# Fewer weight chunks in flight, a later scan of the second batch's v, and a new order of the first transfers

## The chip, the cores and the metric

The kernel runs on one core of one Trainium2 chip. The metric is the device time of one execution in microseconds (us); the number quoted is the median of several executions.

## What is computed

An attention layer whose scores get a learned relative-position bias, followed by a gated feed-forward block. Cut to what matters:

```python
scores = scale * np.matmul(q, k.transpose(0, 1, 3, 2))        # 4 batches, 8 heads, 576 x 576, head_dim 64
psi_rel = np.log1p(np.abs(rel)); psi_i = np.log1p(np.maximum(pos[:, None], 1.0))
h = np.maximum((psi_rel / psi_i)[..., None] @ w1 + b1, 0.0)   # hidden 32
attn = softmax(scores + (h @ w2).transpose(2, 0, 1))          # one bias per head, the same for all batches
x = (attn @ v)                                                # as 2304 tokens x 512
out = ((x @ w_a) * (x @ w_b)) @ w_out                         # d_ff 1536; the weights are float64
```

## The kernel before

All of it is one program on one core. The position bias is made first, in units of 16 query rows, and stored to a buffer in HBM (`bias_d`), from which each attention tile later loads its 128 rows. The first 16 units are made in the opening stage (lines 825 to 831): the log table `u` is scaled by `w1` (line 129), four rectified copies of it are made on VectorE and ScalarE (lines 143 and 147), TensorE contracts them (line 153, tile `psta`), ScalarE evicts (lines 169 and 172) and GpSimd issues the store to `bias_d` (line 174). Ten matmuls on a constant tile (`keep`, line 820, tile `pr`) stand ahead of the first unit on TensorE; the constant is written by one GpSimd memset (line 815).

Attention goes over 160 tiles of up to 128 query rows, n = 0, 1, 2, ... in `attn_steps` (line 615). Tile n's soft-max is issued in step n; the loads for a head pair ("unit" in `attn_steps`) are asked for some tiles ahead of its first tile: q and k six tiles, v four, the preparation of q and k three, and that of v one. The first 12 units (`NF`) use v as it is loaded (`whole`, tile `rvw`); the later ones split it.

For each batch, `v_scale` (line 209) scans the four v tiles of that batch for their largest size: it loads them once more (tile `rv`, two buffers), takes absolute sums on ScalarE (line 220), reduces them on VectorE (line 228), has TensorE turn the result (line 77, tile `vm` to `pr`), and spreads a power-of-two scale two steps later (line 90). `VS` says at which tile each batch's scan begins; for batch 1 it is tile 12, one call a tile, so that its turn on TensorE stands in step 17.

The 24 chunks of `w_a` and `w_b`, 512 KB of float64 each, are loaded and turned into two half-precision parts by `wab_steps` (line 318), interleaved with the attention steps: in its step s, chunk s is converted (line 264 on ScalarE, lines 266, 267 and 270 on VectorE), its size is taken one step later (line 287), and its parts are made seven steps later (lines 304 to 308, GpSimd and ScalarE). The raw chunks have six buffers. `fetch_to` asks for chunks ahead: at step s for all up to number `s + min(6, 3 + s // 2)`, where number s has just been converted.

TensorE's order is written out by hand through `merge`; the other engines' instructions, SyncE's transfers among them, are put in order by a scheduler that simulates the program. `paced` keeps a load behind the bias rows that were asked for last, and `late` keeps work on VectorE, ScalarE and GpSimd behind the newest soft-max instructions. From about 95 us on, the feed-forward matmuls (line 690, tile `ab`; line 739, tile `o`) fill TensorE between the attention tiles.

Of the kernel before, what the change touches and what calls it, by code (L numbers as in the profile page):

```python
# [43 lines left out]
N0 = 4 * NP  # L44
# [1 line left out]
NU0 = TOK // 16  # L46
W0 = 4
NF = 3 * NP
VS = N0 - 4, 2 * N0 - 4, 3 * N0 - 10


@with_exitstack
def attention_moe(ctx, tc, q0d, q1d, kd, vd, idn, wp, wa, wb, wo, lsw, lg, rl, out):
    nc = tc.nc
# [4 lines left out]
    att = ctx.enter_context(tc.tile_pool(name="att", bufs=1))  # L59
# [43 lines left out]
    tab = {}  # L103

    def bias_tables():
        wps = cst.tile([128, 10], F32, name="wps")
        nc.sync.dma_start(out=wps, in_=wp)
        lgs = cst.tile([128, S // 4], F32, name="lgs")
        nc.scalar.dma_start(out=lgs, in_=lg)
        rls = cst.tile([128, NU], F32, name="rls")  # L110
        nc.scalar.dma_start(out=rls, in_=rl)
        w2s = cst.tile([128, 32], F32, name="w2s")
        nc.vector.memset(w2s, 0.0)
        for r in range(4):
            sl = slice(32 * r, 32 * r + 32)
            nc.vector.tensor_scalar(
                out=w2s[sl, 8 * r:8 * r + 8], in0=wps[sl, 2:10], scalar1=-1.0, scalar2=None, op0=ALU.mult
            )
        nc.vector.tensor_scalar(out=lgs, in0=lgs, scalar1=wps[:, 1:2], scalar2=None, op0=ALU.mult)
        tab["w1"], tab["w2"], tab["b1l"], tab["rl"] = wps[:, 0:1], w2s, lgs, rls  # L120

    def bias_windows(pool, tag):
        u = pool.tile([128, S], F32, tag=tag, name="u", bufs=1)
        nc.sync.dma_start(out=u, in_=lsw)
        return u
# [192 lines left out]
    def wab_steps(wt):  # L318
        np_ = FC // 2
        raws, wfs, ms, dgs, rms = {}, {}, {}, {}, {}  # L320

        def fetch(i):
            pool = wtp[0] if i % 2 else wt
            raws[i] = pool, w_load(pool, (wa, wb)[i % 2], i // 2)

        ahead = [0]

        def fetch_to(n):
            for i in range(ahead[0], min(n, 4 * np_)):
                fetch(i)  # L330
                ahead[0] = i + 1

        fetch_to(3)
        yield
        for s in range(4 * np_ + 7):
            p, c = divmod(s - 7, 4)
            if 0 <= p < np_:
                if c == 0:
                    rms[p] = wab_scale(p, pow2_up(dgs.pop(p), 4, "w"))
                with late():  # L340
                    wab_parts(p, c, wfs.pop(s - 7), rms[p])
            p, c = divmod(s - 5, 4)
            if 0 <= p < np_ and c == 0:
                dgs[p] = pow2_down(ms.pop(p), 4, "w")
            if 1 <= s <= 4 * np_:
                p, c = divmod(s - 1, 4)
                if c == 0:
                    ms[p] = wtp[1].tile([128, 4], F32, tag="wm", name="wm", bufs=2)
                wab_size(2 * p + c // 2, c % 2, wfs[s - 1], ms[p])
            if s < 4 * np_:  # L350
                wfs[s] = wab_conv(s, *raws.pop(s))
                fetch_to(s + 1 + min(6, 3 + s // 2))
            yield

    def wo_steps(wt):
# [259 lines left out]
    def attn_steps():  # L615
        vgen = [None]
        for n in range(NT + 3):
            u = TILES[n][0] if n < NT else None
            if n == 0:
                qk_pair(0)  # L620
            if n + 4 < N0:
                load_bias(n + 4)
            elif N0 <= n + 2 < NT:
                load_bias(n + 2)
            if n < NT:
                soft1(n)
            for _ in range(stream[1].count(2 * n)):
                next(stream[0], None)
            for ahead, un in ((a, TILES[n + a][0]) for a in (6, 4, 3, 1) if n + a < NT and FIRST[TILES[n + a][0]] == n + a):
                if un < NP:  # L630
                    continue
                if ahead == 6:
                    load_unit(un)
                elif ahead == 4:
                    b, hp, c = UNITS[un]
                    st["raw", un] = *st["raw", un][:2], load_v(b, hp, whole=un < NF)
                elif ahead == 3:
                    with late():
                        prep_k(un)
                        prep_q(un)  # L640
                else:
                    if un == B * NP:
                        v_tail()
                    with late():
                        prep_v(un)
            if n in VS:
                vgen[0] = v_scale(VS.index(n) + 1)
            if vgen[0]:
                next(vgen[0], None)
            yield  # L650
            for _ in range(stream[1].count(2 * n + 1)):
                next(stream[0], None)
            if n + 1 < N0 + 2:
                if n % 2:
                    qk_pair(n + 1)
            elif n + 1 < NT:
                qk(n + 1, qkp)
            if n == B * N0 + 1:
                chunk_pool(1)
            if n >= 2 and n - 2 < NT:  # L660
                turn(n - 2, tpp)
            if n == N0 + 1:
                pv_first(n - 2, pvp)
            elif n >= 3 and n - 3 < N0:
                if TILES[n - 3][1][0] == "B" and n != N0 + 2:
                    pv_first(n - 3, pvp)
            elif n >= 3 and (n - 2 >= NT or TILES[n - 3][0] != TILES[n - 2][0]):
                pv(TILES[n - 3][0], pvp)
            if 1 <= n <= NT:
                soft2(n - 1)  # L670
            yield
# [131 lines left out]
    with tc.tile_pool(name="bg", bufs=1, side="right") as bg, tc.tile_pool(name="eq", bufs=1, space=PSUM) as eq, \  # L803
            tc.tile_pool(name="prp", bufs=1, space=PSUM) as prp[0]:
        epool[:] = bg, eq
        bias_tables()
        tab["idn"] = cst.tile([128, 128], F32, name="idn")
        nc.scalar.dma_start(out=tab["idn"], in_=idn)
        tab["one"] = wtmp.tile([4, 128], F32, name="one")
        nc.vector.memset(tab["one"], 1.0)  # L810
        uls = bias_windows(att, "rk")
        bias_scale(uls)

        busy = w16t[:, FC - 1, 0, 0].rearrange("p k n -> p (k n)")
        nc.gpsimd.memset(busy, 1.0)

        def keep(n):
            ps = pr_tile()
            for _ in range(n):
                nc.tensor.matmul(ps, busy[:, 0:128], busy, start=True, stop=True)  # L820

        spare = w16t[:, 2:].rearrange("p f j x k n -> p (f j x k n)").bitcast(F32)
        hrows = spare[:, :16 * S].rearrange("p (b g n) -> p b g n", b=4, g=4)

        def first_units(banks):
            for un in range(NU0):
                h4 = hrows[:, un % 4]
                hs = bias_relu(lambda g: h4[:, g], uls, un, int(un % 2 == 0 or un >= 8))
                keep((10, 2, 2, 2, 1, 1, 1)[un] if un < 7 else 0)
                bias_unit(bh, lambda: banks(un), un, hs, 6, nc.gpsimd)  # L830
                yield

        def first_loads():
            for un in range(NP):
                load_unit(un)
                prep_k(un)
                prep_q(un)
                yield
            for un in range(NP):
                b, hp, c = UNITS[un]  # L840
                st["raw", un] = None, None, load_v(b, hp, True)
                prep_v(un)
                yield

        def two(un):
            return (qkp, eq)[un % 2].tile([128, 2, 512], F32, tag="qk", name="psta", bufs=1)

        fl = first_loads()
        ws = ctx.enter_context(ExitStack())
        wtp[0] = ws.enter_context(tc.tile_pool(name="wty", bufs=1, reuse_waits="tile"))  # L850
        with tc.tile_pool(name="bh", bufs=1, side="right") as bh:
            units = first_units(two)
            merge((units, NU0 // 2), (fl, 2 * NP))
            next(wts)
            for m in range(4):
                load_bias(m)
            merge((units, NU0 // 2), (v_scale(0), 7), (wts, 2))
        keep(8)
        merge((asteps, 4), (wts, 1), ((keep(2) for _ in range(4)), 4))
        merge((asteps, 2 * N0 - 10), (wts, 7))  # L860
        n0 = 2 * ends[0] - 2 * N0 + 6
        merge((asteps, n0), (wts, 3), ((keep(2) for _ in range(n0)), n0))
# [32 lines left out]
    with tc.tile_pool(name="bg2", bufs=1, reuse_waits="tile") as bg:  # L895
        uls = bias_windows(bg, "u")
# [70 lines left out]
```

## Time and profile before

| what | value |
|---|---|
| median of 3 runs | 793.14 us (791.31 to 797.51) |
| profiled execution, its own time | 791.7 us |
| its span, from the first to the last instruction | 789.9 us |
| granted TensorE clock, mean | 0.998 |
| TensorE busy | 756.0 us, 96% of the span |
| VectorE, ScalarE, GpSimd busy | 65%, 63%, 41% |
| transfers | 114.15 MB, mean 145 GB/s |

A busy share is a mean over the whole span; a wait in one stage is read from that stage. PE is TensorE's matmuls, PEld its weight loads, DVE VectorE, ACT ScalarE, POOL GpSimd, SP SyncE, which issues most transfers. "Idle before" in a row is the time for which the engine stood still ahead of that instruction, and behind the arrow is what ended it.

### The profile page before, as it was taken

How to read it: one execution, taken by the hardware profiler on the slowest of the kernel's cores; microseconds unless marked ns; L12 is line 12 of the kernel's file. 1: busy time of each engine (PE TensorE's matmuls, PEld its weight loads, DVE VectorE, ACT ScalarE, POOL GpSimd, SP SyncE). 2: the span in 40 equal slices, each digit the busy share in tenths (PEclk: the TensorE clock that was granted, in tenths of full speed). 3: DMA queues.
4: the chain of work that ended last, by engine and by line, in shares of the span. 5: the costliest groups of instructions: out<-in, count | busy, mean ns of one | idle time of the engine just before them, and what ended most of it. 6: DMA issues, size and time to landing. Idle time of an engine off the chain costs nothing.

```text
span 789.9 us, 16363 instructions
## 1 busy us (share of the span) xinstructions
PE 756.0 (96%) x5939; PEld 601.1 (76%) x5939; DVE 509.6 (65%) x1203; ACT 500.1 (63%) x1086; POOL 321.9 (41%) x493
## 2 busy tenths in 40 slices
PE   7778899998999999999999999999999999999998
PEld 1245566677876676888888889888988888888886
DVE  7688688589975787658777877777776662110100
ACT  6879787878866787657775776567666663421310
POOL 3448667946742233224443344234433443320200
PEclk9999999999999999999999999999999999999999
DMA  8999575678645545444444443444344211100001
GB/s 258 319 363 320 181 229 177 200 238 266 200 123 171 159 138 154 122 151 124 125 142 144 145 125 109 129 145 125 109 134 141 77 54 54 48 1 27 2 14 40
DMA packets 52979, 114.15 MB, mean 145 GB/s; under 512 B 6564, under 2 KB 10916, under 8 KB 52900
## 3 DMA queue, kind: packets, MB, share of 16 engines
q1 hardware_dynamic: 45744, 97.35, 39.0%
q10 hardware_dynamic: 5876, 10.93, 4.7%
q0 software_dynamic: 1280, 4.84, 1.8%
q8 instruction: 47, 0.77, 0.4%
q14 instruction: 32, 0.26, 0.1%
HBM read 95.91 MB, written 17.18 MB: 143 GB/s over the span
## 4 chain that ended last, share of the span: by engine, by line
PE 72%; DVE 8%; ACT 6%; issue 4%; DMA 4%; POOL 3%; SPq 1%; ACTq 0%; DVEq 0%; POOLq 0%
PE ab L690 27%; PE o L739 19%; PE qk L468 8%; PE tp L545 8%; PE pv L594 6%; PE psta L153 3%; DVE p L496 2%; DMA bias<-bias_d 2%; ACT p L501 1%; DVE wt L270 1%; DMA rv<-vd 1%; DVE w16t L267 1%; POOL wos L312 1%; DMA rvf<-vd 1%; DVE w16t L266 1%
## 5 line engine op out<-in xcount | busy, mean ns | idle before, releaser
L690 PEld LDWEIGHTS <-w16t 128*128 128x128 f16 x2592 | 250.6, 98 | 41.7 <-issue 13.3
L690 PE MATMUL ab<-x,w16t 128*128 128x256 f16 x2304 | 270.1, 273 | 0.4 <-DVE g L700 0.3
L532 POOL TENSOR_SCALAR p<-p,sm 128x576 f32<-128x576 f32 x144 | 125.9, 874 | 65.3 <-DVE sm L530 57.7
L496 DVE CUSTOM_DVE_ANT_0 p<-qk,bias 128x576 f32<-128x576 f32 x144 | 108.3, 754 | 60.9 <-PE tp L545 55.0
L501 ACT ACTIVATE p<-p,mn 128x576 f32<-128x576 f32 x144 | 111.7, 776 | 40.8 <-DVE mn L496 39.8
L739 PE MATMUL o<-wos,gh 128*128 128x512 f32 x384 | 123.2, 402 | 0.0
L715 POOL TENSOR_TENSOR gl<-g,gh 128x256 fp32r<-128x256 f32 x96 | 71.8, 748 | 121.5 <-ACT gh L714 120.1
L529 POOL TENSOR_SCALAR sm<-sm 128x1 f32<-128x1 f32 x144 | 32.1, 223 | 198.4 <-ACT p L501 194.6
L568 ACT CAST pt<-tp 128x640 f16<-128x640 f32 x96 | 66.3, 691 | 70.8 <-PE tp L545 70.2
L545 PE MATMUL tp<-idn,p 128*128 128x128 f32 x720 | 104.5, 276 | 6.8 <-ACT ptf L550 4.2
L545 PEld LDWEIGHTS tp<-idn,p 128*128 128x128 f32 x720 | 83.4, 141 | 20.6 <-issue 8.4
L700 DVE SCALAR_TENSOR_TENSOR g<-ab,wv,asb 128x256 f32<-128x256 f32 x84 | 40.4, 481 | 79.1 <-ACT asb L698 78.3
L739 PEld LDWEIGHTS o<-wos,gh 128*128 128x128 f32 x384 | 68.9, 188 | 16.2 <-issue 3.3
L468 PE MATMUL qk<-ks,qs 128*128 128x288 f32 x384 | 73.0, 312 | 5.2 <-DVE mn L496 5.1
L739 PE MATMUL o<-wos,gl 128*128 128x512 f32 x192 | 75.4, 393 | 0.0
L468 PEld LDWEIGHTS qk<-ks,qs 128*128 128x128 f32 x384 | 56.6, 190 | 14.3 <-DVE mn L496 7.1
L698 ACT ACTIVATE asb<-ab,wv 128x256 f32<-128x256 f32 x84 | 39.3, 468 | 38.3 <-PE ab L690 38.1
L572 DVE TENSOR_TENSOR pt<-tp,pt 128x512 f16<-128x512 f32 x80 | 55.1, 689 | 8.0 <-ACT pt L568 7.9
L714 ACT CAST gh<-g 128x256 fp32r<-128x256 f32 x96 | 38.8, 404 | 33.9 <-DVE g L700 33.7
L530 DVE RECIPROCAL sm<-sm 128x1 f32<-128x1 f32 x144 | 23.3, 162 | 44.1 <-POOL sm L529 43.1
L400 DVE TENSOR_TENSOR ks<-rk,ks 64x576 fp32r<-64x576 f32 x48 | 44.7, 932 | 4.5 <-ACT ks L399 1.7
L739 PEld LDWEIGHTS o<-wos,gl 128*128 128x128 f32 x192 | 36.0, 188 | 8.2
(107 smaller groups left out, 1033.3 us busy)
## 6 DMA issues: line engine op xcount, KB each, us to landing
bias<-bias_d SPq DMA_DIRECT2D x128, 288.0 KB, 2.9
rv<-vd SPq DMA_DIRECT2D x32, 320.0 KB, 3.3
rk<-kd SPq DMA_DIRECT2D x24, 288.0 KB, 3.4
wraw<-wa SPq DMA_DIRECT2D x12, 512.0 KB, 6.9
wraw<-wb SPq DMA_DIRECT2D x12, 512.0 KB, 5.1
wraw<-wo SPq DMA_DIRECT2D x12, 512.0 KB, 4.3
bias_d<-bo ACTq DMA_DIRECT2D x20, 295.5 KB, 3.0
rq<-q1d SPq DMA_DIRECT2D x16, 320.0 KB, 3.8
```

The lines of the kernel that those rows point to most:

```text
L400: nc.vector.tensor_tensor(out=ks[ol, j], in0=rk[sl], in1=ks[sl, j].bitcast(F32), op=ALU.subtract)
L468: nc.tensor.matmul(ps[:, hf, :HB], a, b[:, hf * HB:hf * HB + HB], start=(x == 0), stop=(x == len(prods) - 1))
L496: ttr = nc.vector.tensor_tensor_reduce(out=p.rearrange("p (a n) -> p a n", a=2), in0=ps[:, :, :HB], in1=bt.rearrange("p (a n) -> p a n", a=2),
L501: exps.append(nc.scalar.activation(p, p, AF.Exp, bias=mn, scale=-1.0, accum_out=sm))
L532: nc.gpsimd.tensor_scalar(out=p, in0=p, scalar1=rc, scalar2=1.0, op0=ALU.mult, op1=ALU.mult)
L545: nc.tensor.transpose(tp[:, x, :], p[:, c0:c0 + 128], tab["idn"])
L568: nc.scalar.copy(dst[:, 0:5], src)
L572: nc.vector.tensor_tensor(out=dst[:, 5:9], in0=src[:, 0:4], in1=dst[:, 0:4], op=ALU.subtract)
L594: nc.tensor.matmul(ps[64 * j:64 * j + 64, :N], v[:, j, :], p[:, j * N:j * N + N], start=(x == 0), stop=(x == len(prods) - 1),)
L690: nc.tensor.matmul(ab[:, j], w16[nm, f][:, pw, kk, :], xs[px][:, kk, :], start=(x % (3 * KC) == 0), stop=(x % (3 * KC) == 3 * KC - 1),)
L715: nc.gpsimd.tensor_tensor(out=gl, in0=g, in1=gh.bitcast(F32), op=ALU.subtract)
L739: nc.tensor.matmul(o, g[:, sl], wos[f][:, p], start=(f == 0 and x == 0), stop=(f == FC - 1 and x == 2))
```

## The change

Four edits. The log table is loaded ahead of everything else on SyncE's queue; the small table `wps` moves from SyncE's to ScalarE's queue, ahead of `lg` and `rl`; and the identity matrix, which came third on ScalarE's queue, is issued by GpSimd. The scan of the second batch's v starts at tile 14 in place of tile 12. Weight chunks are asked for at most 4 steps ahead in place of 6 (the formula differs from step 4 on). The v tiles of units 4 to 11 are asked for three tiles ahead in place of four.

```diff
-VS = N0 - 4, 2 * N0 - 4, 3 * N0 - 10
+VS = N0 - 2, 2 * N0 - 4, 3 * N0 - 10
...
-        nc.sync.dma_start(out=wps, in_=wp)
+        nc.scalar.dma_start(out=wps, in_=wp)
...
-                fetch_to(s + 1 + min(6, 3 + s // 2))
+                fetch_to(s + 1 + min(4, 3 + s // 2))
...
                 if ahead == 6:
                     load_unit(un)
-                elif ahead == 4:
+                elif ahead == (4 if un >= NF else 3):
                     b, hp, c = UNITS[un]
                     st["raw", un] = *st["raw", un][:2], load_v(b, hp, whole=un < NF)
-                elif ahead == 3:
+                if ahead == 3:
                     with late():
                         prep_k(un)
                         prep_q(un)
-                else:
+                elif ahead == 1:
...
+        uls = bias_windows(att, "rk")
         bias_tables()
         tab["idn"] = cst.tile([128, 128], F32, name="idn")
-        nc.scalar.dma_start(out=tab["idn"], in_=idn)
+        nc.gpsimd.dma_start(out=tab["idn"], in_=idn)
         tab["one"] = wtmp.tile([4, 128], F32, name="one")
         nc.vector.memset(tab["one"], 1.0)
-        uls = bias_windows(att, "rk")
         bias_scale(uls)
```

## Rows read from the trace of the kernel before

**Rows 1.** Busy time of each engine over the whole span.
```profile
PE 756.0 (96%) x5939; PEld 601.1 (76%) x5939; DVE 509.6 (65%) x1203; ACT 500.1 (63%) x1086; POOL 321.9 (41%) x493
```
**Rows 2.** Busy time by stage, clock, share of the transfer engines, GB/s.
```profile
28.00:100.00 72.00, 60.18 (x463) 35.66 (x464) 51.17 (x149) 57.86 (x136) 42.96 (x63) 1.00 0.84 291
100.00:230.00 130.00, 122.13 (x949) 94.52 (x946) 107.27 (x241) 102.56 (x224) 91.30 (x109) 0.99 0.67 211
230.00:670.00 440.00, 438.51 (x3569) 367.23 (x3566) 315.90 (x727) 291.68 (x622) 156.23 (x279) 1.00 0.42 126
```
**Rows 3.** The same view in stretches of 6 us: PE, PEld, DVE, ACT, POOL.
```profile
70.00:76.00 6.00, 5.67 (x52) 3.44 (x48) 4.38 (x15) 5.59 (x16) 4.53 (x7) 1.00 0.99 330
76.00:82.00 6.00, 5.21 (x39) 2.87 (x36) 4.51 (x15) 6.00 (x16) 3.63 (x7) 1.00 0.82 285
82.00:88.00 6.00, 4.89 (x38) 2.78 (x37) 4.00 (x13) 3.87 (x10) 3.97 (x6) 1.00 0.61 201
```
**Rows 4.** Timeline of the start: us from the start, duration, instruction, idle before.
```profile
0.75 0.39 SPq L107 DMA_DIRECT2D wps<-wp  x1
1.20 0.42 SPq L124 DMA_DIRECT2D u<-lsw  x1
1.32 3.84 PE L820 MATMUL pr<-w16t 128*128 128x512 f16 x10 [1.32 <-POOL w16t L815]
...
3.37 0.30 DVE L119 TENSOR_SCALAR lgs<-lgs,wps 128x144 f32<-128x144 f32 x1
4.34 0.52 DVE L129 TENSOR_SCALAR u<-u,wps 128x576 f32<-128x576 f32 x1 [0.68 <-DMA u<-lsw]
...
5.48 1.54 PE L153 MATMUL psta<-w16t,w2s 128*32 128x288 f32 x8 [0.32 <-DVE w16t L143]
```
**Rows 5.** GpSimd's transfer issues: first one, all 16 (ns min/median/max); VectorE beside it.
```profile
L174 POOL DMA_DIRECT2D bias_d<-bo x1: 4222/4222/4222, 9.5 to 9.5; - x1
L174 POOL DMA_DIRECT2D bias_d<-bo x16: 530/575/4222, 9.5 to 35.0; - x16
4.90 8.65 DVE L143 TENSOR_SCALAR w16t<-u,lgs 128x576 f32<-128x576 f32 x21
```
**Rows 6.** Timeline around the end of batch 1's scan.
```profile
78.75 0.38 SPq L205 DMA_DIRECT2D rv<-vd  x1
...
84.22 0.74 ACT L220 ACTIVATE rv<-rv 128x640 f32<-128x640 f32 x1 [1.30 <-DMA rv<-vd]
84.86 0.19 ACT L220 ACTIVATION_READ_ACCUMULATOR rv<-rv 128x1 f32 x1
85.39 0.38 PE L77 MATMUL pr<-idn,vm 128*1 128x128 f32 x2 [0.74 <-DVE vm L228]
86.13 0.59 PE L820 MATMUL pr<-w16t 128*128 128x512 f16 x2 [0.37 <-DVE p2m L79]
```
**Rows 7.** Weight chunks: SyncE's wait (us, times, longest), VectorE's wait, landing times, conversions.
```profile
SPq L258 <- DVE w16t L267: 16.0, 12, 2.5
...
48.40 0.76 DVE L496 CUSTOM_DVE_ANT_0 p<-qk,bias 128x576 f32<-128x576 f32 x1 [1.92 <-DMA bias<-bias_d]
...
DMA to landing us min/median/max: 3.8/5.7/11.9
...
DMA to landing us min/median/max: 4.5/4.6/5.2
...
115.48 1.11 DVE L267 SCALAR_TENSOR_TENSOR w16t<-wraw,w16t 128x512 int32<-128x512 int32 x1
126.24 0.67 ACT L264 ACTIVATE wt<-wraw 128x512 f32<-128x512 f32 x1
```
**Rows 8.** The first use of a moved v tile on TensorE.
```profile
111.50 2.53 PE L594 MATMUL pv<-ptw,rvw 128*64 128x256 f32 x20
```
**Rows 9.** One stall of TensorE at 195 us, and its stretch by the stage view.
```profile
195.60 1.33 PE L468 MATMUL qk<-ks,qs 128*128 128x288 f32 x4 [2.58 <-DVE mn L496]
...
195.00:200.00 5.00, 4.40 (x24) 3.91 (x25) 3.95 (x11) 4.42 (x10) 3.82 (x5) 0.66 0.76 262
```

## Prediction

> **What bounds the kernel now.** I read the engines' totals first, then the busy time by stage, then the chain of waits and the timeline of the stages that the edits touch. TensorE is busy for 96% of the span [rows 1], and the stage view says where the rest is: from 230 to 670 us it is busy 438.51 us of 440, so nothing that is done to transfers there can be bought back; from 100 to 230 us it lacks 7.9 us, and from 28 to 100 us it lacks 11.8 us [rows 2]. The edits act between 0 and 135 us, so the most they could give is a part of those 11.8 and 7.9 us and of the opening. What is saved early passes on to the end, since later work follows in a fixed order on TensorE; what is saved inside another engine's slack is lost. The transfers are near full between 34 and 76 us (a share of 0.99 in 70 to 76) and far from full after 82 us (0.61) [rows 3]. That picture suits the change, but a full transfer queue costs only where an engine stands waiting for it. In all of 28 to 260 us only two waits of an engine over half a microsecond were ended by a transfer: VectorE once 1.92 us for bias rows [rows 7], and ScalarE once 1.30 us for a v tile [rows 6]. That small sum is why I expect little.
>
> **The opening.** The log table's issue moves from 1.20 to 0.75 us on SyncE [rows 4], 0.45 earlier. VectorE waits for that table now (0.68 us ahead of 4.34). The table `lg` goes the other way: it was first on ScalarE's queue and is second now, one issue of 0.45 later. VectorE's instruction on it at 3.37 did not wait, so `lg` had landed by then; at worst it lands at 3.82, and with that instruction's 0.30 us the table is scaled from 4.12 on. So the scaling starts 0.22 to 0.45 us earlier, and the first real matmul, at 5.48 behind VectorE, could start at 5.03 to 5.26. But the ten constant matmuls stand ahead of it on TensorE and end at 1.32 + 3.84 = 5.16 [rows 4], which leaves a gain of 0.2 to 0.3. The constant comes from GpSimd, and the identity's issue now stands ahead of that memset in the program. The trace shows no identity issue on GpSimd; the nearest rows are its 16 bias stores, which hold it for 0.53 us at least and 0.575 in the median, with one of 4.22 [rows 5]. At 0.53 to 0.75 the ten matmuls end at 5.69 to 5.91, 0.2 to 0.4 us later than the first real matmul starts today. If the scheduler puts the memset first, it is -0.3; if the issue takes 4.22 us, the ten matmuls end at 9.38, and it is 9.38 - 5.48 = +3.9. I take +0.3, by the median row, because 4.22 has a cause beside it that is missing at 0.75 us: VectorE ran without a gap from 4.90 to 13.55, and that store, begun at 9.45, ended at 13.67 [rows 5]. The moves of `wps` and `rl` cost nothing: `wps` is issued at the same 0.75 us, and `rl` is first used by the eviction behind the first `psta` matmuls.
>
> The page SBUF — State Buffer of the Trainium skill (section "SBUF: two separate sides") has a rule on this: a transfer issued by GpSimd has its descriptors written by GpSimd itself, and VectorE can lock it out of the port that it needs for that until VectorE's instruction is done. The 4.22 us store beside VectorE's run agrees with it. By that rule the identity's issue is a short one and the sum below stands at -1.7; by the reading that GpSimd's first issue is slow in itself, the sum is +1.9.
>
> **The scan of batch 1's v, two tiles later.** Today its last tile is asked for at 78.75 us and read from 84.22 on, 5.4 us later; ScalarE waits 1.30 us for it; TensorE, whose order is fixed, waits 0.74 us for the reduced result and 0.37 us for its small successor [rows 6]. Two tiles later the loads fall where the transfer share is 0.61 at most [rows 3], so I count both waits as gone: -1.1 us (bounds 0 and -1.1). What TensorE meets next is the score matmul of the following tile, whose operands have been there long. Second, ScalarE is the fullest engine between 70 and 82 us, 11.59 us of 12, and idle for 2.1 us of the 6 behind that [rows 3]. The other three of the four absolute sums lie in the full stretch, each like the fourth, 0.74 + 0.19 = 0.93 us [rows 6]. Two of them move out: 1.9 us of ScalarE's work goes to where it has room. The chain there changes between ScalarE, VectorE, GpSimd and TensorE, so I count half, -0.9 us (bounds 0 and -1.9). The scale itself is ready in step 21 in place of 19, and its first reader is the eviction behind the matmuls at 111.50 [rows 8], in the second half of step 22: covered, by less than two steps. Were that cover gone, VectorE and TensorE would wait a few tenths of a microsecond there.
>
> **Chunks at most 4 steps ahead.** It removes no transfer; from step 4 on each chunk is asked for up to two steps later. With 6 ahead and 6 buffers, SyncE stands at each request until the chunk just being converted has been read: 16.0 us in 12 waits [rows 7]. With 4 ahead that buffer has been free for two steps, so these waits go. Queued behind them are bias rows and v tiles, but their readers hardly wait, so I count 0. It could be better by the 1.92 us that VectorE waited for bias rows [rows 7]; against that, the rows which landed at 48.3 were issued at 39.2, before the first chunk that moves (asked for near 45 us). It could be worse where steps are shortest: the chunk converted at 126.24 would be asked for once the conversion at 115.48 has ended at 116.59, 9.65 us before its use. Landings take 5.2 us at most after 95 us, and 11.9 at most in the full stretch [rows 7]: cover of 4.4 us, or a loss of 2.3 at the worst. I take 0, as the late rows are the nearer ones.
>
> **v of units 4 to 11, one tile later.** Each is asked for ten tiles ahead of its first matmul (four ahead of its unit, used six into it), where that of the first stands at 111.50 [rows 8]; one tile less is covered many times over, and from unit 6 on the load waits for its buffer anyway. It is 0.
>
> **The sum.** +0.3 - 1.1 - 0.9 + 0 + 0 = -1.7 us. Against the profiled execution that is 791.7 - 1.7 = 790.0 (span 788.2). The median of the runs lies 1.4 above it, so 793.14 - 1.7 = 791.4.
>
> **The rivals.** (a) GpSimd's first issue is slow in itself: in place of +0.3 it is +3.9, the sum is +1.9, 795.0, slower than before. It decides from an issue of about 2.2 us on, where the opening eats the other two gains. For it: the only first issue in the trace took 4.22. Against it: that issue ended when VectorE's run did. (b) The scheduler's new order removes the stall at 195 us. There VectorE did weight conversions ahead of a soft-max step, TensorE stood for 2.58 us, and then ran in a stretch with a granted clock of 0.66, that is, part of it at the lower level of 1.2 GHz; its four score matmuls took 1.33 us for the usual 0.77, and with the five transposes and 36 feed-forward matmuls behind them some 1.7 us more were lost [rows 9]. Without it: -4.3, 787.1. (c) The same in the other direction: the order of conversions puts one more such stall there: 795.7. Nothing in the edits aims at 195 us, so both are chance. (d) The scan's waits only move with it to step 19, where feed-forward matmuls queue behind them: the -1.1 is not had, 792.5. Against it: the transfers are half idle there. (e) The chunk edit opens the full stretch between 34 and 76 us after all, VectorE's 1.92 us go: 789.5.
>
> **How the numbers follow.** Chances: the forecast 0.45, (a) 0.13, (b) 0.13, (c) 0.11, (d) 0.10, (e) 0.08. The forecast's own range is 788.5 to 794.0. The range for all must take in (b) with some of (e) below and (c) above, and the runs of one kernel reach from 791.31 to 797.51 by themselves: 785.5 to 797.0. A change of 1%, 7.9 us, is about what a measurement of this kernel can tell from none. Faster than that needs (b), (e) and the full 1.9 us of ScalarE together: 0.08. Slower than that needs (a), (c) and a late chunk together: 0.05. Same: 0.87.
>
> **What the profile will show.** Right: the first `psta` matmul between 5.1 and 5.9 us; GpSimd's identity issue near 0.6 us; no wait of TensorE at line 77 for `vm`, whose turn comes near 94 us; two absolute sums fewer before 82 us; SyncE's waits at line 258 for line 267 nearly gone; TensorE still at about 756 us busy. Wrong: a `psta` near 9 us, a wait for `wraw` at line 264, `vm` still waited for, or TensorE's idle time between 100 and 230 us off by several microseconds, which would be the order of VectorE and not the edits' own waits.

## The result: slower, and the profile after

The changed kernel takes 799.16 us (median of 15 runs, 794.75 to 801.37) against 793.14 us for the kernel before (15 runs, 790.94 to 797.51): a ratio of 1.0065, with a 95% interval of 1.0048 to 1.0082, that is 5.2 us more (3.8 to 6.5). Forecast were 791.4 us and a range of 785.5 to 797.0, so the sign was wrong, and the time lies above the range. The profiled execution of the changed kernel took 800.78 us, 9.1 more than the one of before; it lies near the top of its kernel's runs, so its trace shows more of the loss than the median has.

The engines' totals, and the busy time by stage with the clock in the seventh column, answer to [rows 1, 2]; the stretches of 10 us stand ahead of the three stages.

```profile
PE 763.1 (96%) x5939; PEld 604.3 (76%) x5939; DVE 508.8 (64%) x1203; ACT 500.4 (63%) x1086; POOL 324.6 (41%) x494
```

```profile
10.00:20.00 10.00, 5.22 (x40) 0.96 (x36) 5.51 (x15) 6.72 (x19) 5.29 (x3) 0.83 0.97 333
...
50.00:60.00 10.00, 7.02 (x36) 4.05 (x32) 4.48 (x15) 5.68 (x14) 1.87 (x4) 0.66 0.83 294
60.00:70.00 10.00, 9.13 (x73) 6.35 (x71) 7.72 (x21) 8.02 (x20) 5.32 (x8) 0.82 0.77 254
70.00:80.00 10.00, 7.25 (x62) 5.32 (x61) 8.09 (x22) 8.56 (x20) 8.92 (x12) 0.86 0.82 252
...
28.00:100.00 72.00, 58.94 (x415) 33.93 (x416) 46.92 (x134) 54.98 (x131) 41.93 (x58) 0.91 0.82 279
100.00:230.00 130.00, 122.96 (x937) 93.39 (x936) 106.97 (x248) 102.09 (x221) 91.13 (x109) 0.99 0.67 212
```

TensorE ran the same 5939 matmuls and was busy 7.1 us longer. The stage rows show a lower granted clock in 10 to 20 us and from 50 to 80 us, where the trace of the kernel before had 1.00 throughout; the twenty `pv` matmuls at 59.77 us took 2.60 us there in place of 1.46. In 28 to 100 us it did 415 matmuls in place of 463, while its busy time fell by only 1.2 us. From 100 to 230 us the row is nearly that of before, so most of the time went early.

The places where one instruction stands for the same work show how the lag grew. First before, then after: the last constant matmuls of the opening, the `pv` matmuls that stand at 57.99 us before, the score matmul that stands at 120.27 us before, behind the turn of `vm` in both kernels, and, of after alone, that turn.

```profile
33.62 1.90 PE L820 MATMUL pr<-w16t 128*128 128x512 f16 x8
57.99 1.46 PE L513 MATMUL pv<-ptf,rvf 128*64 128x128 f32 x20
120.27 1.24 PE L468 MATMUL qk<-rkf,rqf 64*128 64x288 f32 x4
```

```profile
35.83 1.90 PE L820 MATMUL pr<-w16t 128*128 128x512 f16 x8
66.36 1.46 PE L513 MATMUL pv<-ptf,rvf 128*64 128x128 f32 x20
101.95 0.38 PE L77 MATMUL pr<-idn,vm 128*1 128x128 f32 x2
...
127.99 1.24 PE L468 MATMUL qk<-rkf,rqf 64*128 64x288 f32 x4
```

The changed kernel is 2.2 us late at the end of the opening, 8.4 at 58 us, and 7.7 at 120 us. `vm` is turned at 101.95 us with no wait, where it waited 0.74 before [rows 6]; that is a part of what came back, and the experiment on the scan alone has the rest.

What happened in the opening stands in the timeline, whose first rows answer to [rows 4]:

```profile
0.74 0.42 ACTq L107 DMA_DIRECT2D wps<-wp  x1
...
1.28 0.76 POOL L809 DMA_DIRECT2D idn<-idn  x1 [0.83 <-POOLq L958]
...
2.64 3.73 PE L820 MATMUL pr<-w16t 128*128 128x512 f16 x10 [2.64 <-POOL w16t L815]
...
3.99 0.69 DVE L116 TENSOR_SCALAR w2s<-wps 32x8 f32<-32x8 f32 x4 [2.96 <-DMA wps<-wp]
...
6.30 0.60 PE L153 MATMUL psta<-w16t,w2s 128*32 128x288 f32 x2
...
13.40 0.74 ACT L220 ACTIVATE junk<-rvf 128x640 f32<-128x640 f32 x1 [2.35 <-DMA rvf<-vd]
...
14.13 0.47 ACT L169 ACTIVATE bo<-psta,rls 128x272 f32<-128x272 f32 x1
14.50 0.72 ACT L220 ACTIVATE junk<-rvf 128x640 f32<-128x640 f32 x1
...
15.60 0.29 ACT L172 ACTIVATE bo<-psta,rls 128x47 f32<-128x47 f32 x1
...
15.95 1.08 PE L153 MATMUL psta<-w16t,w2s 128*32 128x256 f32 x8 [3.02 <-ACT bo L172]
...
53.30 0.76 DVE L496 CUSTOM_DVE_ANT_0 p<-qk,bias 128x576 f32<-128x576 f32 x1 [2.32 <-DMA bias<-bias_d]
54.12 2.29 PE L482 MATMUL qk<-rkf,rqf 64*128 64x288 f32 x6 [2.63 <-DVE mn L496]
```

The first `psta` matmul is 0.8 us late. The larger thing comes at 13.40: ScalarE stands for 2.35 us for the first v tile of batch 0's own scan (line 220, tile `rvf`). The eviction of a finished `psta` tile (line 169) starts only once that scan is through. A second scan follows at 14.50, and the eviction that TensorE waits for, at 15.60 (line 172), stands behind both: by 15.95 TensorE has waited 3.02 us. In the program's order on ScalarE, before above and after below, the first two scans have moved ahead of three evictions each:

```
before:  L169 288 | L172 31 | L169 272 | L169 288 | L172 47 | L220 | L169 256 | L147 | L220
after:   L169 288 | L172 31 | L220 | L169 272 | L220 | L169 288 | L172 47 | L220 | L169 256 | L147 | ...
```

GpSimd's stores, in the view of [rows 5]:

```profile
L174 POOL DMA_DIRECT2D bias_d<-bo x16: 530/534/4229, 10.0 to 39.2; - x16
```

The slowest store takes what it took before, and the last one is issued at 39.2 us in place of 35.0. None of the four edits touches batch 0's scan. The scheduler, which simulates the program to order ScalarE's work, placed it elsewhere. The Trainium skill, page PSUM — Partial Sum Buffer (section "Engine vs sequencer instructions"), says that ScalarE's queue is strictly first in, first out; the rows agree: the eviction stood behind the scan, and began at 14.13 as the scan that had started at 13.40 ended.

### The profile page after: what moved, and what is told of

It reads as the page before. It is cut to its first block, busy times and chain, and to the rows that moved or that the text cites. A ratio compares the mean times of both kernels' runs of the same rounds, so it can differ in the third digit from the quotient of the medians.

```text
span 798.8 us, 16370 instructions
## 1 busy us (share of the span) xinstructions
PE 763.1 (96%) x5939; PEld 604.3 (76%) x5939; DVE 508.8 (64%) x1203; ACT 500.4 (63%) x1086; POOL 324.6 (41%) x494
## 4 chain that ended last, share of the span: by engine, by line
PE 73%; DVE 8%; DMA 5%; ACT 5%; issue 4%; POOL 3%; SPq 0%; ACTq 0%; DVEq 0%; POOLq 0%
PE ab L690 27%; PE o L739 19%; PE tp L545 8%; PE qk L468 8%; PE pv L594 5%; DMA bias<-bias_d 3%; PE psta L153 3%; DVE p L496 2%; DVE wt L270 1%; ACT p L501 1%; DVE w16t L267 1%; DMA bias_d<-bo 1%; PE pv L513 1%; DVE ks L400 1%; PE qk L482 1%
```

## The experiments

My theory was this order on ScalarE. The rivals were the later requests (scan, chunks, v tiles), the late constant on TensorE and the late small table, and the lower clock by itself. Each ratio below is against runs of the kernel before on the same chip, with its 95% interval; 0.001 is 0.8 us.

**The opening's edits alone, and the later requests alone.**

```diff
e1: only the hunks of bias_tables and of the opening (wps, idn, uls)
e2: only VS, min(4, ...) and the v tiles
```

> Only the three edits of the first transfers. Theory A: the identity's issue holds GpSimd for 0.76 us ahead of the constant, the scheduler therefore sets the scan of the first batch's v ahead of the bias evictions on ScalarE, ScalarE waits over 2 us there for a v tile, and the bias chain, TensorE's clock and the first bias rows pay for it: 6 to 9 us slower than before (799 to 802), a wait of ScalarE of over 1.5 us at line 220 and first score matmuls 2 us or more later. Theory B, the rival: the loss lies in the later requests (chunks, v tiles, scan), and the opening costs only its 0.3 to 0.8 us: 793 to 794.

> Only the scan two tiles later, chunks 4 steps ahead and the v tiles one tile later; the opening as before. Theory A: 1 to 2 us faster than before (791 to 792), as the prediction's sum without its opening. Theory B: most of the loss, 797 to 799.

The opening alone: 798.69 us, ratio 1.0053 (1.0028 to 1.0079); in its profile ScalarE waits 1.50 us for the first scan's v tile, and TensorE 2.17 us behind it. That profile is of the fastest of its nine runs, 793.80 us: TensorE is 2.8 us late at the end of the opening (the constant matmuls of 33.62 us stand at 36.37) and hardly later after that, and the clock in 50 to 60 us is 1.00, where the changed kernel had 0.66:

```profile
12.59 0.74 ACT L220 ACTIVATE junk<-rvf 128x640 f32<-128x640 f32 x1 [1.50 <-DMA rvf<-vd]
...
15.14 0.64 PE L153 MATMUL psta<-w16t,w2s 128*32 128x256 f32 x8 [2.17 <-ACT bo L172]
...
50.00:60.00 10.00, 7.46 (x61) 4.57 (x57) 7.99 (x24) 8.93 (x23) 3.73 (x8) 1.00 0.98 357
```

The later requests alone: 793.83 us, 1.0006 (0.9989 to 1.0024). Its trace, with the order of before on ScalarE in the opening, has a long stretch at the lower clock all the same:

```profile
50.00:60.00 10.00, 9.59 (x53) 6.27 (x51) 7.23 (x21) 6.40 (x16) 3.98 (x7) 0.61 0.69 220
```

The loss is the opening's, and the three later edits together are worth nothing that these runs can tell.

**The identity behind the constant.** The whole change, with GpSimd's identity issue one line further down:

```diff
-        nc.gpsimd.dma_start(out=tab["idn"], in_=idn)
...
         nc.gpsimd.memset(busy, 1.0)
+        nc.gpsimd.dma_start(out=tab["idn"], in_=idn)
```

> The whole change, with the identity's issue set behind the constant's memset on GpSimd instead of ahead of it. ScalarE's order in the opening is then the one of before. Theory A: the loss is gone, 791 to 793.5, and no wait at line 220 over 0.5 us. Theory B: as slow as the whole change, about 798 to 799.

794.15 us, ratio 1.0007 (0.9987 to 1.0026): the loss is gone. The scans stand in the order of before, and the first waits for nothing at 13.67 us. The first `psta` matmul still comes at 6.14 us, held by VectorE, since `wps` is as late here as in the changed kernel. So the late small table is not the loss. (This kernel has the later scan's gain too, so being level doesn't show that the table costs nothing.)

**The scan held back.** Moving the identity changes both the constant's time and the order. To part them, the whole change, identity ahead of the constant and all, with each scan of batch 0 held behind the evictions that it stood behind before (`bos` is the list of the evictions):

```diff
-            with late():
+            with late() if b else tc.issue_after(bos[(7, 8, 10, 10)[hp]].ins):
```

> The whole change, identity ahead of the constant, but the scan of the first batch's v held on ScalarE behind the same evictions as before. It tells ScalarE's order from the 0.76 us of GpSimd itself. If the order is the cause: 792 to 795, with the first bias matmul still near 6.3 us. If the late constant itself is the cause: 798 to 799.

794.21 us, ratio 1.0007 (0.9981 to 1.0034). In its timeline, where line numbers are one higher than in the changed kernel from line 188 on, and in its stage view:

```profile
2.64 3.71 PE L821 MATMUL pr<-w16t 128*128 128x512 f16 x10 [2.64 <-POOL w16t L816]
6.28 1.23 PE L153 MATMUL psta<-w16t,w2s 128*32 128x288 f32 x8
...
13.50 0.73 ACT L221 ACTIVATE junk<-rvf 128x640 f32<-128x640 f32 x1
...
10.00:20.00 10.00, 6.79 (x66) 1.52 (x62) 7.77 (x22) 8.33 (x22) 5.96 (x4) 1.00 0.94 332
...
50.00:60.00 10.00, 8.01 (x75) 5.51 (x73) 9.69 (x25) 8.49 (x21) 4.42 (x8) 1.00 0.84 291
```

The constant matmuls are as late as in the changed kernel (2.64 us) and the first `psta` matmul too (6.28), yet ScalarE waits for no v tile, the clock is 1.00 in both stretches, and the loss is gone. It is the order on ScalarE and not the lateness of the constant. This is the nearest pair of the study: TensorE, GpSimd and SyncE run the same instructions in the same order as in the changed kernel. Apart from the scans, the traces differ in the place of one weight chunk's size pass on ScalarE and, from 17.5 us on, of some conversion steps on VectorE. The ratios lie 0.0058 apart, 4.6 us.

**The identity alone, in the kernel before.**

```diff
-        nc.scalar.dma_start(out=tab["idn"], in_=idn)
+        nc.gpsimd.dma_start(out=tab["idn"], in_=idn)
```

> The kernel before, with one edit: the identity issued by GpSimd, ahead of the constant's memset. The scheduler then sets the scan of the first batch's v ahead of the bias evictions, as in the whole change. If that order is enough for the loss: 4 to 7 us slower than before, with a wait of over 1 us at line 220. If the late small tables and log table have a part in it: 0 to 3 us slower.

799.8 us, ratio 1.0074 (1.0051 to 1.0097): one moved issue makes the whole loss. Its rows are those of the changed kernel:

```profile
13.17 0.74 ACT L220 ACTIVATE junk<-rvf 128x640 f32<-128x640 f32 x1 [2.45 <-DMA rvf<-vd]
...
15.78 0.80 PE L153 MATMUL psta<-w16t,w2s 128*32 128x256 f32 x8 [3.18 <-ACT bo L172]
...
10.00:20.00 10.00, 5.15 (x44) 1.12 (x44) 4.85 (x13) 6.91 (x18) 4.64 (x3) 0.81 0.92 322
...
50.00:60.00 10.00, 9.13 (x44) 5.90 (x42) 4.50 (x13) 4.99 (x11) 2.88 (x6) 0.50 1.02 393
```

**Each later request by itself.**

```diff
e6:
-VS = N0 - 4, 2 * N0 - 4, 3 * N0 - 10
+VS = N0 - 2, 2 * N0 - 4, 3 * N0 - 10
e7:
-                fetch_to(s + 1 + min(6, 3 + s // 2))
+                fetch_to(s + 1 + min(4, 3 + s // 2))
```

> The kernel before, with the second batch's scan two tiles later and nothing else. Theory A (the gain is real and given back at the conversions): the wait at line 77 for the scan near 85 us is gone, the score matmuls near 91 us are 1 to 2 us earlier, and TensorE waits longer than 0.88 us for the turn of the weights' sizes near 123 us; the time is within 1 us of before. Rival (it is not given back there but eaten by the chunk edit): 1.5 to 2 us faster, 791.5 to 792.

> The kernel before, with chunks at most 4 steps ahead and nothing else. If a cover of 4 steps is enough: within 1 us of before, no wait for a raw chunk, and SyncE's waits at line 258 for line 267 down from 16 us to under 10. If requests come too late: 1.5 to 4 us slower, with ScalarE waiting for raw chunks.

The scan alone: 791.38 us (790.32 to 797.01), ratio 0.9973 (0.9951 to 0.9995), about 2.1 us faster, which is the time of the rival. The chunks alone: 793.86 us, 0.9993 (0.9973 to 1.0013), no difference. The scan's rows, in the kernel with the scan alone and then in the kernel before: `pv` matmuls ahead of the scan, the turn of `vm` (of the first kernel alone), a score matmul behind it, the turn of a weight chunk's size, and a later score matmul.

```profile
71.41 1.46 PE L513 MATMUL pv<-ptf,rvf 128*64 128x128 f32 x20
...
94.39 0.38 PE L77 MATMUL pr<-idn,vm 128*1 128x128 f32 x2
...
120.43 1.24 PE L468 MATMUL qk<-rkf,rqf 64*128 64x288 f32 x4
...
124.17 0.38 PE L77 MATMUL pr<-idn,wm 128*4 128x128 f32 x2 [1.81 <-ACT w16t L287]
...
148.79 1.23 PE L468 MATMUL qk<-rkf,rqf 64*128 64x288 f32 x4 [0.46 <-DVE mn L496]
```

```profile
69.69 1.46 PE L513 MATMUL pv<-ptf,rvf 128*64 128x128 f32 x20
...
120.27 1.24 PE L468 MATMUL qk<-rkf,rqf 64*128 64x288 f32 x4
...
123.09 0.38 PE L77 MATMUL pr<-idn,wm 128*4 128x128 f32 x2 [0.88 <-ACT w16t L287]
...
148.58 1.23 PE L468 MATMUL qk<-rkf,rqf 64*128 64x288 f32 x4 [1.50 <-DVE mn L496]
```

`vm` is no longer waited for. The profiled execution (span 790.1) is no faster as a whole than that of before, since its clock fell between 44 and 51 us; the `pv` matmuls at 71.41 are 1.72 us late, the score matmul at 120.43 only 0.16. So the scan's gain can be seen in the trace as well: 1.56 us. Of it 1.1 come between 84 and 95 us and 0.4 between 72 and 76. The turn of a weight chunk's size near 124 us waits 0.93 us longer, but that is not lasting: ahead of the score matmul at 148 us the kernel before waits 1.04 us longer in its turn, and the two are 0.21 apart again. The traces of the changed kernel and of e2, e3 and e4, which hold the later scan too, make up 1.5 to 1.9 us between 72 and 95 us, while e2, e3 and e4 are no faster than before by their medians.

In the chunk run SyncE's wait at its requests fell as forecast, from 16.0 us [rows 7] to 7.7, and the time did not change:

```profile
SPq L258 <- DVE w16t L267: 7.7, 6, 2.1
```

**Fewer chunks in flight at the start.** The profiles of most of these kernels show a wait of VectorE for bias rows near 48 us, from 0.7 to 3.5 us long, and in several of them the clock is lower near it. If chunk transfers make those rows late, asking for fewer chunks there takes the wait away. The later requests alone (e2), with

```diff
-                fetch_to(s + 1 + min(4, 3 + s // 2))
+                fetch_to(s + 1 + min(4, 2 + s // 4))
```

> Opening as before, scan, v tiles and chunks as in the change, but min(4, 2 + s // 4) ahead in place of min(4, 3 + s // 2): two to three chunks of 512 KB fewer are asked for ahead of the bias rows for which VectorE waits near 48 us. If those chunks are what the rows stand behind: that wait (1.9 to 2.9 us so far) falls under 0.5 us, TensorE's clock stays at its upper level there, and the time is 2 to 4 us shorter than before (789 to 791), with less scatter. If it is not: within 1 us of before.

792.35 us, ratio 0.998 (0.9958 to 1.0002): inconclusive as a time. The wait for bias rows was gone from the profile, but the clock fell all the same, to a mean of 0.81 in 44 to 62 us, so the clock falls there without that wait too. Nor does it always fall with it: the kernel before waits 1.92 us there [rows 7] and e3 2.25, both with the clock at 1.00.

```profile
44.00:62.00 18.00, 15.05 (x117) 10.61 (x118) 14.13 (x38) 13.60 (x33) 6.31 (x13) 0.81 0.80 281
```

**Matmuls that only fill.** TensorE's gaps in that stretch were filled with one matmul on the constant tile behind each of 22 attention steps, once beside the scan alone (e9), once in the whole change (e10):

```diff
-        merge((asteps, 2 * N0 - 10), (wts, 7))
+        merge((asteps, 2 * N0 - 10), (wts, 7), ((keep(1) for _ in range(2 * N0 - 10)), 2 * N0 - 10))
```

> The scan of the second batch's v two tiles later, all else as in the kernel before, and one matmul on the constant tile behind each of the 22 attention steps that run from about 39 to 85 us (work that the result doesn't need). TensorE's short waits for the softmax there are then partly filled. If the granted clock falls in that stretch because TensorE stands still too often, the clock is now 1.00 in 40 to 60 us, the runs of this kernel lie within about 1 us of each other in place of 790.32 to 797.01, and the median is 790 to 791, no worse than the 791.38 of the same kernel without them. If the fall comes from the one long wait for bias rows, the clock falls as before; the fillers then cost what of them lies outside idle time, 2 to 4 us, and the median is 793 to 795.

> The whole change, the identity's issue ahead of the constant included, and the same 22 matmuls on the constant tile from about 41 to 93 us. If most of the loss between 50 and 80 us is the lower clock, the clock comes back sooner after the wait for bias rows, and the median falls from 799.2 to about 795 to 797. If the loss is made of the waits themselves (the v tile, the rows), the clock helps little, the fillers take time of their own, and the median is 799 to 803.

Both missed. Beside the scan: 799.18 us, ratio 1.0054 (1.003 to 1.0077), against 0.9973 without the fillers, so they cost 0.0081, 6.4 us. In the whole change: 803.47 us, 1.012 (1.0092 to 1.0148), 4 us more than without. The stage view with fillers, and then without, both with the scan alone:

```profile
40.00:64.00 24.00, 20.38 (x147) 11.77 (x145) 18.10 (x48) 17.35 (x41) 10.29 (x18) 1.00 0.92 331
...
70.00:80.00 10.00, 7.10 (x39) 4.05 (x40) 7.72 (x18) 6.94 (x16) 6.92 (x10) 0.66 0.82 278
```

```profile
40.00:64.00 24.00, 19.31 (x138) 12.89 (x136) 19.11 (x51) 18.36 (x44) 11.10 (x18) 0.86 0.92 330
```

The clock was 1.00 in 40 to 64 us as the first theory had it (it then fell in 70 to 80), and still the kernel was slower. The fillers are 22 times 0.38 us, 8.4 us by their durations, and 6.4 of it came out as time. VectorE's 3.32 us wait for bias rows stayed too. Where the time went stands in the same two traces, with fillers and then without:

```profile
66.58 1.46 PE L513 MATMUL pv<-ptf,rvf 128*64 128x128 f32 x20
...
74.18 0.58 PE L820 MATMUL pr<-w16t 128*128 128x512 f16 x1 [1.79 <-DVE p2m L79]
...
79.89 1.24 PE L482 MATMUL qk<-rkf,rqf 64*128 64x288 f32 x8
```

```profile
65.60 1.46 PE L513 MATMUL pv<-ptf,rvf 128*64 128x128 f32 x20
...
73.33 1.24 PE L482 MATMUL qk<-rkf,rqf 64*128 64x288 f32 x8
```

Up to 66 us the kernel with fillers is only 1.0 us behind the one without; at the turn of a weight chunk's size it is 2.2 behind (72.01 us against 69.80), and at the score matmul of 79.89 it is 6.6. In between TensorE stands 1.79 us at a filler, which writes the tile `pr`: that tile has one buffer (line 71), and VectorE has yet to read the turned size of a weight chunk from it (line 79). The clock then is at its lower level for a while, 0.66 in the mean of 70 to 80. The whole change with fillers has the same wait, 1.83 us at 79.04. So in this trace a third of the price comes ahead of that wait, and the rest with it and with the low clock behind it; fillers with a buffer of their own were not run. The pair doesn't measure what the lower clock costs, since the fillers add a price of their own.

## Why the prediction was wrong

**The opening, forecast at +0.3: the step that failed.** Alone it cost 4.2 us (2.2 to 6.3). I costed the identity's issue on GpSimd as its own 0.53 to 0.75 us plus the matmuls behind it, and let everything else keep its order. As a duration that was right: 0.76 us, and rival (a) fell, since GpSimd's first issue is not slow in itself; the slow one is again the first store beside VectorE's run (4.23 us). By the rule that the prediction took from the Trainium skill, page SBUF — State Buffer (section "SBUF: two separate sides"), an issue without VectorE's long run beside it is a short one, and the 0.76 us agree. What I left out is that the scheduler orders the other engines by a simulated clock: an issue of 0.76 us on GpSimd moved two absolute sums on ScalarE ahead of evictions that TensorE needs. Behind them TensorE waited 3.02 us. Restoring that order took the loss away (e4), and the identity alone made it (e5). Rivals (b) and (c) did price new orders, but at 195 us only, where there was a stall to look at, and not in the stage that was being edited. (By its own rows rival (a) would have decided from an issue of 2.3 us on, 2.0 + 5.48 - 5.16, and not from about 2.2.)

I also had the small table at nothing, "issued at the same 0.75 us". It was issued at 0.74, and VectorE waited for it until 3.99 in place of 2.64 us. It cost some 0.7 us on the first `psta` matmul (e3). What of it lasts is not shown: the two kernels with that delay and the old order, e3 and e4, are level with the kernel before, but they hold the scan's gain as well.

**How about 3 us became more.** By the traces, TensorE's wait leaves it late at the end of the opening by 2.2 us in the changed kernel, 2.8 in e1 and 3.3 in e5 (36.90 us against 33.62). The rest, up to 8.4 us in the changed kernel's trace, is added between 37 and 66 us. There TensorE waits 2.63 us ahead of the score matmul at 54.12, behind VectorE's 2.32 us for bias rows (in the kernel before the two waits are 0.79 and 1.92 us), and then the clock is low until 63 us. This second part is not tied to the order in every execution: e1's trace has the order and adds 0.2 us there, and e2's has the order of before and loses about 4 us between 45 and 56 us, at a clock of 0.61 in 50 to 60. Shown by the medians is that the loss as a whole goes with the order on ScalarE.

How much of it is clock can be estimated, since the mean granted clock of every run is on record. In the 32 runs of the kernel before beside e1, 0.01 of mean clock goes with 4.7 us, and in the 29 beside e5 with 4.0. The runs of e1 and of e5 have a mean clock 0.005 lower than those of before (0.988 against 0.993, 0.987 against 0.992). That makes some 2.3 us of mean differences of 4.6 and 5.7 us; the 2 to 3.5 us left are about what TensorE has lost by the end of the opening. This is an estimate from the scatter of the runs: no run here held the clock fixed.

**The scan, forecast at -1.1 and -0.9: right in kind, its second term too large in the trace.** Alone it gave 2.1 us by the medians (0.4 to 3.9) where the sum said 2.0. By the trace it is 1.5: the two waits, counted at 1.1, gave 1.1, and ScalarE's relief, counted at 0.9, gave no more than the 0.4 us between 72 and 76 us. That the median comes so near to 2.0 is partly luck. `vm` was not waited for, and rival (d), the waits moving along to step 19, fell. The forecast that the scale would be ready in time held as well.

**The chunks, forecast at 0: right.** 0.9993 with an interval of some 1.7 us to either side; SyncE's wait fell from 16.0 to 7.7 us and nobody had stood behind it. No late chunk was seen, and rival (e) fell. **The v tiles, forecast at 0**, were not run by themselves.

**Three later edits, forecast at -2.0, gave +0.5 (-0.9 to +1.9).** That is 2.6 us short of the scan alone, with a difference whose interval only just leaves out zero. e2's trace does hold the scan's gain, 1.5 us between 72 and 95 us, and loses more than that at the lower clock before. Whether the chunks or the v tiles have a part in that, or the two medians lie at opposite ends of their intervals, is open.

**The stall at 195 us** stayed, and moved along: 2.57 us ahead of a score matmul at 204.31 in the changed kernel. Rivals (b) and (c) didn't happen as they were told.

**The range.** Its upper end was made of single mishaps, 4.3 us above the forecast at most (rival (c)), with the scatter of the runs on top, and held no case in which the opening loses a few microseconds to a new order and the next stage adds to them. The change lies within 1%, which had most of the chance.

The fastest of the measured versions by its median is the scan alone, 0.9973 of the kernel before and about 0.991 of the changed one.

## What to carry to other kernels

Where a scheduler orders the engines by simulated time, any edit that shifts an early instruction, even an issue of 0.8 us on an idle engine, must be costed as a possible new order on every other engine; compare the order of the instructions before and after, and look first for work that waits on a transfer and now stands ahead of work that TensorE needs. Work that has slack, such as a scan whose result is read much later, can be held behind the urgent evictions by an explicit order, as in e4. Put a new issue behind what the critical engine waits for on that queue, as in e3. Look at the buffer that a filling matmul writes, too: here it was shared, and TensorE stood 1.79 us for its reader.

## What was not expected of the hardware

A 5 KB table (`wps`), issued at 0.74 us on ScalarE's queue at the same moment as the 288 KB log table on SyncE's, was there for VectorE at 3.99 us; issued at 0.75 us with the log table 0.45 us behind it on the same queue it was there at 2.64 [rows 4]. Which of the differences does it (the queue, the order, the other transfers under way) was not tried apart.

Filling TensorE did not pay here: with 22 matmuls of 0.38 us the granted clock in 40 to 64 us was 1.00 in place of 0.86, the two levels being 1.2 and 2.4 GHz, and the kernel lost 6.4 us. These are the clocks of one profiled execution each, and the trace of the kernel before had 1.00 there without fillers.
